# Transforms on 64 by 64 parts of TensorE's array, in one burst a group

## The chip, the cores and the metric

The kernel runs on one core of one Trainium2 chip. A core has a matrix engine (TensorE, PE in the profile, with its weight loads shown as PEld), a vector engine (VectorE, DVE), a scalar engine (ScalarE, ACT), a general engine (GpSimd, POOL) and SyncE (SP), which here only issues DMA transfers. The metric is the device time of one execution in microseconds. All data are 32-bit floats.

## What is computed

The reference filters a sequence in the frequency domain and feeds the result to a gated feed-forward block:

```python
X = np.fft.rfft(x, axis=1)              # x: 8 batches, 3008 tokens, 256 channels
Y = X * (filt_r + 1j * filt_i)[None]    # one complex factor for each of 1505 frequencies and channel
y = np.fft.irfft(Y, n=3008, axis=1)
t = y.reshape(8 * 3008, 256)
g = t @ w_gate                          # w_gate, w_val: 256 by 1536; w_out: 1536 by 256
out = (g / (1 + exp(-g)) * (t @ w_val)) @ w_out
```

The weights arrive as 64-bit floats, which the kernel rounds to 32 bits itself during the first batch.

## The kernel before

**Two streams of work.** The feed-forward part of batch b runs in 12 groups (four chunks of 752 tokens, three slices of the hidden units each, `NCHUNK` and `NG`). In the same groups the transform of batch b + 1 is made, so that it is ready when batch b ends. The last batch, having no follower, transforms nothing.

**The feed-forward part** multiplies with fewer products than the plain method takes. Sums of inputs (`y_t`) and sums of weights (`wt_t`) stand in for some of the products, and operations of VectorE, ScalarE and GpSimd put the results together. Its products are at L862 (PSUM tiles `wk`, `wa`, `we`: 188 columns) and, for the output projection, at L954 (`wA`, `wF`, `wG`: 376 columns). [...] Seven are one pool (`wps`, `bank`) that the feed-forward tiles use in turn, and one is apart (`fps`, `fbank`) and serves the transform.

**The transform** splits 3008 into 47 by 64. The first step makes a real 47-point transform for each of the 64 columns, 24 complex frequencies (48 numbers) each. The middle step takes, for each of the 24 frequencies, a 64-point transform with the twiddle factors in its matrix (128 by 128, for real and imaginary parts of 64 values), multiplies with the filter, and goes back with a second 128 by 128 matrix. The last step is 47 points back. Between the steps the data go through DRAM (`d1`, `d2`), which changes what lies on the 128 partitions.

From batch 2 on, the first step uses that the inputs of a real transform can be paired: `pair` (VectorE) makes sums and differences of rows n and 47 - n, and `stage1_paired` (L639, L641) takes five columns at once with a table of 120 rows and columns, 13 times. The middle step has 12 units (`stage2a`, `stage2b`), each for two frequencies: two matmuls of 128 by 128 by 256 columns at L698, three VectorE operations with the filter at L707, L711 and L714 (each reading PSUM), one addition on GpSimd (L716, shown at its helper's line, L256), two matmuls back at L731, one ScalarE copy (L739) and a transfer to `d2`. The filter is loaded for each unit from its inputs, in six transfers of 64 KB (L580). Batches 0 and 1 have transforms of their own: batch 0 before the groups begin, batch 1 (`stage1`, L658) during the groups of batch 0. The last step (`stage3`, L765) is made in groups 0, 1, 4, 7 and 11.

**The order is written out by hand.** The string `SCHEDULE` lists the operations of a group as tokens, and every instruction is put on its engine in that order (`pin`). [...] P, Q, A, B and E are products, W projections (those of the group before), f, c, x, s, y, e, m, l, g, u, h, v the operations between and after the products, S and D are GpSimd's, and o and z put projections into the output. A token `t2.1` is the place for piece 2, part 1 of the transform: a list `plan` says which units of the transform are the pieces of a group, and a unit is a Python generator whose parts run at successive tokens. A group thus has up to five pieces.

Of the kernel before, what the change touches and what calls it, by code (L numbers as in the profile page):

```python
# [41 lines left out]
FP32 = mybir.dt.float32  # L42
U32 = mybir.dt.uint32
# [15 lines left out]
NH = 4  # L59
# [13 lines left out]
NP = 5  # L73
NPAIR = N1 // 2
N_PAIRED = -(-N2 // NP)

# [12 lines left out]
Q0 o3' z1.o' t4.2' W2 f0 S00' S01' x0.o' t0.0 x1.o' Q1 t0.1 x2.o' P3 x3.o' f1 t4.3' W1 x4.o' S10' x03 S11'  # L89
s13 x5.o' P1 o1 t0.2 P0 o2 z0.o c1 D01 A13 g1 c0 S20' Q2 S21' g0 y01 m13 t1.0 h0 f2 s01 W6 t1.1 h1 x23  # L90
D02 P2 o6 D12 A01 c2 B13 g2 n3' m01 t0.3 S30' t1.2 x02 W7 S31' g13 y12 y02 B01 h13 o7 t1.3 t2.0 s02
s12 g01 h2 Q3 t2.1 h01 e12 A02 y23 W4 e02 y03 m02 g3 A12 o4 z2.o t2.2 E12 m12 B02 t2.3 l12 E02 u12 e13
g02 t3.0 h3 s23 l02 B12 v12 E13 t3.1 h02 u02 A23 n2 l13 g12 v02 W5 s03 e23 h12 e01 m23 A03 o5
# [8 lines left out]
""".split()  # L102
BLOCKS = (0, 1, 3, 2)
# [21 lines left out]
def dft_tables():  # L125
# [31 lines left out]
    paired = np.zeros((NP * (NPAIR + 1), 2, NP, NS))  # L157
    for j in range(NP):
        paired[NPAIR * j:NPAIR * (j + 1), :, j] = w[1:NPAIR + 1]
        paired[NP * NPAIR + j, 0, j] = 1.0  # L160
    paired = paired.reshape(NP * (NPAIR + 1), -1)


    pairs = np.arange(128).reshape(2, N2).T.ravel()
    later = np.stack([de[:, :, 0], de[:, :, 1][:, :, pairs]], 2)
    f32 = np.float32
    return (wf.reshape(NR, NK).astype(f32), wi.reshape(NK, NR).astype(f32),
            back.astype(f32), paired.astype(f32), np.ascontiguousarray(de).astype(f32),
# [4 lines left out]
def kernel(  # L173
# [11 lines left out]
    wf_host, wi_host, back_host, paired_host, de_host, later_host = dft_tables()  # L185
    wf_dram = nc.inline_tensor(wf_host, name="wf_tbl")
    wi_dram = nc.inline_tensor(wi_host, name="wi_tbl")
    paired_dram = nc.inline_tensor(paired_host, name="paired_tbl")
# [34 lines left out]

    def weights_of(b, k, g):
        return wt_1 if b == 0 and k < NT and g == 1 else wt_t
# [6 lines left out]
    w_dram = wdpool.tile([NG, 128, NPR, 2, 128], FP32, name="w_all")  # L232
    wo_t = cpool.tile([128, NJ, 7, 128], FP32)
# [19 lines left out]
    pin = tc.keep_in_program_order  # L253

# [3 lines left out]
    def sub(eng, dst, a, b):  # L258
        return eng.tensor_tensor(out=dst, in0=a, in1=b, op=ALU.subtract)  # L259
# [224 lines left out]
    back_t, paired_t, differences, third = [], [], [], []  # L484

    def load_back():

        for n in range(3):
            t = rpool.tile([128, 2, 128], U32, name=f"paired_{n}", tag="pw", bufs=3)
            t = t.bitcast(FP32).rearrange("p b f -> p (b f)")  # L490
            (differences if n else paired_t).append(t[0:NP * (NPAIR + (not n))])
        t = rpool.tile([128, 2, 128, 2], U32, name="x_third", tag="raw", bufs=2)
        t = t.bitcast(FP32).rearrange("p b f two -> p (b f two)")
        third.append(t[0:NP * (NPAIR + 1)].rearrange("p (i c) -> p i c", c=C))
        pin(nc.sync.dma_start(out=paired_t[0][:, 0:2 * NP * NS], in_=paired_dram.ap()))
        t = rpool.tile([128, 2, 128, 2], U32, name="back", tag="raw", bufs=2)
        t = t.bitcast(FP32).rearrange("p b f two -> p (b f two)")
        back_t.append(t[:, 0:10 * N1])
        pin(nc.sync.dma_start(out=back_t[0], in_=back_dram.ap()))
# [15 lines left out]
    class Spectral:  # L515
# [25 lines left out]
        def load_x(self, u):  # L541
            if self.b == 0:
                rows = x[0].rearrange("(r n) c -> r n c", n=32)
                for a, n in ((0, 4), (4, 4)):
                    for r in (slice(0, 80), slice(80, NR)):
                        self.load(out=x0[u][r, a:a + n, :],
                                  in_=rows[r, 8 * u + a:8 * u + a + n, :])
            elif self.b > 1:
                if u < N_PAIRED:
                    t = third[0]  # L550
                    if u % 3 < 2:
                        t = xpool.tile([NP * (NPAIR + 1), 2, C], FP32, name=f"x_{self.b}_{u}",
                                       tag="x")
                    n2, pairs = min(NP * u, N2 - NP), NP * NPAIR
                    rows = x[self.b].rearrange("(n1 n2) c -> n2 n1 c", n2=N2)
                    back = bass.AP(tensor=x.tensor,
                                   offset=x.offset + ((self.b * N1 + N1 - 1) * N2 + n2) * C,
                                   ap=[[C, NP], [-N2 * C, NPAIR], [1, C]])
                    self.load(out=t[0:pairs, 0], in_=rows[n2:n2 + NP, 1:NPAIR + 1])
                    self.load(out=t[0:pairs, 1], in_=back)  # L560
                    self.load(out=t[pairs:pairs + NP, 0], in_=rows[n2:n2 + NP, 0])
                    self.x[u] = t
            elif u < N_ONE:
                self.x[u] = xpool.tile([NR, NV, C], FP32, name=f"x_{self.b}_{u}", tag="x")
                rows = x[self.b].rearrange("(r n) c -> r n c", n=32)

                for r in (slice(0, 80), slice(80, NR)):
                    self.load(out=self.x[u][r], in_=rows[r, ts(u, NV), :])

        def load_two(self, u):  # L570
            if u < N_TWO:
# [10 lines left out]
                if self.b < 2:  # L582
                    self.load(out=self.t2[u], in_=self.twos(self.d1, u))
                    return
                rows = self.d1.rearrange("a n c -> (a n) c").rearrange(
                    "(n s p) c -> p n s c", n=N2, p=2)
                for i in range(2):
                    self.load(out=self.t2[u][N2 * i:N2 * (i + 1)], in_=rows[i, :, ts(u, NV)])
# [37 lines left out]
        def pair(self, u):  # L626

            if u < N_PAIRED:
                a, b = [self.x[u][0:NP * NPAIR, i] for i in range(2)]
                pin(sub(nc.vector, differences[u % 2], a, b))  # L630
                pin(add(nc.vector, a, a, b))

        def stage1_paired(self, u):

            t1 = t1pool.tile([NP * NS, 2, C], FP32, name=f"t1_{self.b}_{u}", tag="t1", bufs=2)
            ps = self.bank(f"pa_{self.b}_{u}")[0:NP * NS]
            table = paired_t[0]
            m = NP * NS
            pin(nc.tensor.matmul(out=ps[:, 0], lhsT=table[:, 0:m], rhs=self.x.pop(u)[:, 0],  # L639
                                 start=True, stop=True))  # L640
            pin(nc.tensor.matmul(out=ps[:, 1], lhsT=table[0:NP * NPAIR, m:2 * m],  # L641
                                 rhs=differences[u % 2], start=True, stop=True))
            self.load_x(u + 3)
            yield
            pin(nc.scalar.copy(out=t1, in_=ps))
            n2 = min(NP * u, N2 - NP)

            rows = self.d1.rearrange("a n c -> (a n) c").rearrange("(r p) c -> r (p c)", p=2)
            pin(nc.scalar.dma_start(out=rows[NS * n2:NS * (n2 + NP)],
                                    in_=t1.rearrange("p i c -> p (i c)")))  # L650
            yield
            self.pair(u + 2)
# [444 lines left out]
    older = before = None  # L1097
    pieces_before = []
# [52 lines left out]
    for b in range(B):  # L1151
# [8 lines left out]
        if b:  # L1160
            one = [nxt.stage1_paired(u) for u in range(N_PAIRED)] if nxt else []
        else:
            one = [nxt.stage1(u) for u in range(N_ONE)]
        two = []
        for u in range(N_TWO + 2) if nxt else ():
            two += [nxt.stage2b(u - 2)] if u > 1 else []
            two += [nxt.stage2a(u)] if u < N_TWO else []
        if nxt:
            plan[0] = one[0:2] + d[0][0:1] + one[2:3] + d[0][1:2]
            plan[1] = one[3:4] + d[0][2:3] + one[4:5] + d[0][3:4] + one[5:6]  # L1170
            plan[2], plan[3] = (one[6:10], one[10:13]) if b else (one[6:11], one[11:16])
            plan[4] = d[1] + two[0:1]

            plan[5], plan[6] = [iter(())] + two[1:5], two[5:10]
            plan[7] = two[10:11] + d[2]
            plan[8], plan[9] = two[11:16], two[16:21]
            plan[10], plan[11] = two[21:24], three(nxt, 0)
# [10 lines left out]
        for step in range(NCHUNK * NG + (b == B - 1)):  # L1188
# [16 lines left out]
            for place, token in enumerate(SCHEDULE):  # L1205
# [5 lines left out]
                if op[0] == "t":  # L1211
                    n = int(op[1])
                    ps = pieces_before if old else pieces
                    if n < len(ps):
                        next(ps[n], None)
                elif op[0] in "Wo" or op.endswith(".o"):
# [10 lines left out]
                if nxt and (step, op) == ((4, "P2") if b else (5, "A23")):  # L1227
                    nxt.load_two(0)
                if b + 2 < B and (step, op) in ((10, "Q2"), (10, "B01"), (11, "Q2")):

                    following.load_x(2 if step == 11 else int(op == "B01"))
                if b + 2 < B and step == 11 and op in ("A02", "B02"):
                    following.pair(int(op == "B02"))
# [43 lines left out]
```

## Time and profile before

The median of three runs is 2894.39 us (2893.86 to 2896.27). The profiled execution has a span of 2893.4 us, at a granted TensorE clock of 0.998 of full speed.

| what | value |
|---|---|
| chain of work that ended last | TensorE 89%, GpSimd 3%, VectorE 2% |
| DMA | mean 193 GB/s; 396368 packets, 201080 of them under 512 bytes |
| matmuls L639 and L641 (first step, batches 2 to 7) | 156 and 156 records, means of 379 and 378 ns |
| matmuls L698 and L731 (middle step, batches 1 to 7) | 336 and 336 records, means of 379 and 383 ns |
| copies L645 and L739 on ScalarE | 78 and 84, means of 586 and 585 ns |
| L707, L711, L714 on VectorE | 84 each, means of 691, 693 and 684 ns |
| additions of 128 by 512 on GpSimd (middle step) | 84, mean 1273 ns |
| pairs on VectorE, `x<-x`, `paired<-x`, `x_third<-x_third`, `paired<-x_third` | 54, 54, 24, 24; 36.6, 31.6, 27.9 and 16.7 us in all |

A row of the profile's groups names the line, the engine, the operation and the tiles (out<-in), then the shape and the number of records, the busy time in us, the mean of one in ns, and the idle time of the engine before them with what ended it. [...] the next one starts before it ends, so durations of matmuls do not add up to the time they take.

### The profile page before, as it was taken

Reading aid. Unit: us, or ns where it says so; the run is one execution under the profiler, and the core shown is the slowest. Engines: PE = TensorE matmul, PEld = TensorE weight load, DVE = VectorE, ACT = ScalarE, POOL = GpSimd, SP = SyncE. Lnnn points to the kernel's source line nnn. Section 1 sums busy time; section 2 is a strip of 40 time slices with the busy share of each in tenths; the row PEclk is TensorE's granted clock in tenths of the full one; section 3 lists DMA queues with packets and bytes.
Section 4 is the critical chain, followed back from the end, with each engine's and each line's share of the span. In section 5 each row is a group of like instructions: output and inputs, shape, how many; then the busy total and the mean of one; then the engine's idle time right before and its main releaser. Section 6 shows DMA issues by size and latency. Waiting matters only on the chain.

```text
span 2893.4 us, 47312 instructions
## 1 busy us (share of the span) xinstructions
PE 2843.6 (98%) x14784; PEld 2434.4 (84%) x14784; DVE 2073.4 (72%) x4664; ACT 1576.6 (54%) x4190; POOL 1532.2 (53%) x1669
## 2 busy tenths in 40 slices
PE   8999989999999999999999999999999999999998
PEld 6777778888888888888888888888888888888886
DVE  6888766776777767777767677677677767766666
ACT  6776445555555555555555554555555555555553
POOL 4886665454445554446453555444554544555443
PEclk9999999999999999999999999999999999999999
DMA  8687865666566665667656566566765666645443
GB/s 228 216 264 253 287 193 164 188 211 204 185 182 189 220 190 182 194 185 214 196 179 199 177 213 204 179 196 180 213 192 190 185 207 193 208 140 163 145 138 80
DMA packets 396368, 558.89 MB, mean 193 GB/s; under 512 B 201080, under 2 KB 296586, under 8 KB 396118
## 3 DMA queue, kind: packets, MB, share of 16 engines
q1 hardware_dynamic: 366533, 506.80, 57.7%
q10 hardware_dynamic: 27792, 45.72, 4.7%
q0 software_dynamic: 1792, 3.34, 0.4%
q8 instruction: 120, 1.97, 0.3%
q14 instruction: 131, 1.07, 0.1%
HBM read 460.38 MB, written 95.34 MB: 192 GB/s over the span
## 4 chain that ended last, share of the span: by engine, by line
PE 89%; POOL 3%; DVE 2%; issue 1%; ACT 0%; DMA 0%; POOLq 0%; DVEq 0%
PE wa L862 24%; PE wA L954 16%; PE wk L862 15%; PE we L862 12%; PE wG L954 8%; PE wF L954 4%; PE pd L765 3%; PE pc L731 3%; PE pb L698 2%; PE pa L639 1%; PE pa L641 1%; POOL out_dram L943 1%; POOL h L259 1%; POOL h L256 0%; DVE o L256 0%
## 5 line engine op out<-in xcount | busy, mean ns | idle before, releaser
L862 PE MATMUL wa<-y_t,wt_t 128*128 128x188 f32 x4464 | 879.0, 323 | 9.3 <-DVE wa L884 6.2
L862 PEld LDWEIGHTS wa<-y_t,wt_t 128*128 128x128 f32 x4464 | 748.7, 190 | 90.7 <-ACT wa L888 9.5
L256 POOL TENSOR_TENSOR h<-h 128x376 f32<-128x376 f32 x190 | 184.4, 992 | 778.1 <-DVE h L909 778.1
L862 PEld LDWEIGHTS wk<-y,wt_t 128*128 128x128 f32 x2976 | 501.0, 190 | 80.0 <-DVE y L256 0.5
L862 PE MATMUL wk<-y,wt_t 128*128 128x188 f32 x2976 | 565.0, 323 | 0.0
L259 POOL TENSOR_TENSOR h<-h 128x376 f32<-128x376 f32 x570 | 562.6, 1009 | 0.1
L954 PE MATMUL wA<-h,wo_t 128*128 128x376 f32 x1536 | 549.9, 480 | 9.0 <-POOL h L259 4.6
L862 PE MATMUL we<-y_t,wt_t 128*128 128x188 f32 x2232 | 431.6, 323 | 0.8 <-ACT we L893 0.7
L259 DVE TENSOR_TENSOR we<-we,m 128x376 f32<-128x376 f32 x576 | 316.5, 554 | 136.6 <-PE we L862 87.2
L954 PEld LDWEIGHTS wA<-h,wo_t 128*128 128x128 f32 x1536 | 279.3, 190 | 115.9 <-POOL h L259 8.6
L862 PEld LDWEIGHTS we<-y_t,wt_t 128*128 128x128 f32 x2232 | 369.4, 190 | 1.4 <-ACT we L893 1.0
L259 POOL TENSOR_TENSOR D<-f,f 128x376 f32<-128x376 f32 x288 | 280.9, 987 | 131.7 <-ACT f L877 123.2
L897 ACT COPY m<-wa 128x376 f32<-128x376 f32 x576 | 271.8, 472 | 86.7 <-PE wa L862 83.8
L263 DVE SCALAR_TENSOR_TENSOR y<-wk,c 128x376 f32<-128x376 f32 x480 | 243.7, 540 | 84.6 <-ACT we L893 56.0
L904 ACT ACTIVATE u<-we 128x188 f32<-128x188 f32 x576 | 188.7, 328 | 191.1 <-DVE we L259 171.2
L954 PE MATMUL wG<-h,wo_t 128*128 128x376 f32 x768 | 274.0, 479 | 1.2 <-DVE o L256 1.2
L904 ACT ACTIVATE g<-wa 128x188 f32<-128x188 f32 x576 | 187.3, 326 | 158.9 <-PE wa L862 143.2
L877 ACT ACTIVATE f<-wk 128x376 f32<-128x376 f32 x288 | 139.2, 483 | 223.7 <-PE wk L862 158.3
L881 ACT COPY c<-wk 128x376 f32<-128x376 f32 x288 | 136.0, 472 | 220.8 <-PE wk L862 220.8
L884 DVE SCALAR_TENSOR_TENSOR x<-wk,f 128x376 f32<-128x376 f32 x192 | 104.2, 543 | 201.7 <-PE wk L862 199.6
L893 ACT COPY we<-y 128x376 f32<-128x376 f32 x480 | 221.2, 479 | 39.6 <-DVE h L909 25.5
L909 DVE TENSOR_TENSOR h<-wa,g 128x188 f32<-128x188 f32 x576 | 196.4, 345 | 31.2 <-ACT g L904 30.3
(157 smaller groups left out, 3855.3 us busy)
## 6 DMA issues: line engine op xcount, KB each, us to landing
wt_t<-w_all SPq DMA_DIRECT2D x174, 896.0 KB
wt_t<-w_all SPq DMA_DIRECT2D x174, 768.0 KB
lent<-later_tbl SPq DMA_DIRECT2D x84, 256.0 KB
lent<-in_filt_r_dram SPq DMA_DIRECT2D x336, 64.0 KB
d<-lent ACTq DMA_DIRECT2D x84, 256.0 KB
d<-t ACTq DMA_DIRECT2D x78, 240.0 KB
lent<-d SPq DMA_DIRECT2D x144, 128.0 KB
t<-d SPq DMA_DIRECT2D x112, 128.0 KB
```

The source lines that it names most:

```text
L256: return eng.tensor_tensor(out=dst, in0=a, in1=b, op=ALU.add)
L259: return eng.tensor_tensor(out=dst, in0=a, in1=b, op=ALU.subtract)
L263: return nc.vector.scalar_tensor_tensor(out=dst, in0=a, scalar=-1.0, in1=b, op0=ALU.mult, op1=ALU.subtract)
L862: pin(nc.tensor.matmul(out=ps[:, z], lhsT=self.wt[:, SLOT[p], z], rhs=rhs, start=start and z == 0, stop=True, skip_group_check=True))
L877: pin(act.mul(self.small(f"f{i}", f"f{i}", 1), t[f"k{i}"], -1.0))
L881: pin(act.copy(out=self.small(f"c{i}", f"c{i}", 1), in_=t[f"k{i}"]))
L884: pin(v.scalar_tensor_tensor(out=dst, in0=t[f"k{j}"], scalar=-1.0, in1=t[f"f{i}" if j == 3 else f"D{at}"], op0=ALU.mult, op1=ALU.add))
L893: pin(act.copy(out=self.bank(f"e{at}"), in_=t[f"y{at}"]))
L897: pin(act.copy(out=self.small(f"m{at}", "m", 4), in_=t[f"a{at}"]))
L904: pin(act.activation(out=self.small(op, "g", 3, 1)[:, 0], in_=ps[:, 1], func=AF.Silu))
L909: pin(v.tensor_tensor(out=dst, in0=ps[:, 0], in1=g, op=ALU.mult))
L954: pin(nc.tensor.matmul(out=self.tiles[at], lhsT=wo_t[:, JB * q + i, WO[p], :], rhs=self.hs[i][:, HID[p]], start=start and i == 0, stop=Tru ...
```

## The change

The transforms of batches 2 to 7 are made in another way, and at other places of the order.

- **First step** (`quads`, groups 0 to 3). The 64 columns are taken as two halves, one on partitions 0 to 46, the other on 64 to 110. A tile of the array of 64 rows by 64 columns serves each half with its own 47 by 48 table (`quad`; that of the second half includes a turn). Two tiles of columns next to each other in the array take different columns of the input. The input comes in eight pieces of eight columns, two a group, which make eight matmuls of 512 columns each group, into four PSUM banks.
- **Middle step** (`fours`, groups 4 to 10). `halves` (VectorE) makes the sum and the difference of the two halves of 64 points; from these, the even and the odd of the 64 frequencies come with 64 by 64 matrices instead of one of 128 by 128. A unit has four of the 24 first-step frequencies: eight matmuls of 256 columns there into two banks and, one group later, eight home from two banks, joined by a subtraction and an addition on VectorE.
- **Filter product.** The results of the way there are copied to SBUF (ScalarE). Real and imaginary rows alternate there, and two DMA transfers exchange them into a second tile; VectorE multiplies both tiles with the filter's two parts (`tensor_tensor` and `scalar_tensor_tensor`), GpSimd adds.
- **Filter in DRAM.** `keep_filter` writes the filter once, early in batch 1, into a DRAM tile in the layout wanted (16 transfers). A unit then loads its part in one transfer of 1 MB.
- **Places.** Twelve tokens b0 to b11 in `SCHEDULE` run the parts of a group's burst: all its matmuls at b0, right behind W2 at the head of the group. The banks are of the shared pool of seven. The pieces t0 to t4 hold only the last step from batch 1 on.

The purpose is to let four 64 by 64 matmuls share the array, and to do the middle step with half the multiplications. The core of the diff:

```diff
-Q0 o3' z1.o' t4.2' W2 f0 S00' S01' x0.o' t0.0 x1.o' Q1 t0.1 x2.o' P3 x3.o' f1 t4.3' W1 x4.o' S10' x03 S11'
+Q0 o3' z1.o' t4.2' W2 b0 f0 S00' S01' b1 b2 x0.o' t0.0 x1.o' Q1 t0.1 x2.o' P3 x3.o' f1 t4.3' W1 x4.o' S10' x03 b3 S11'
...
+        def quads(self, g):
...
+                for cp in range(2):
+                    for h in range(2):
+                        r = slice(64 * h, 64 * h + N1)
+                        pin(nc.tensor.matmul(
+                            out=banks[u, h][64 * cp:64 * cp + 64], lhsT=quad_t[0][r, 0:64],
+                            rhs=xt[r, 2 * cp:2 * cp + 2].rearrange("p n c -> p (n c)"),
+                            start=True, stop=True))
...
+        def halves(self, e):
...
+            f = (add, sub)[e]
+            pin(f(nc.vector, self.sums[:, e], t[:, :, 0], t[:, :, 1]))
...
+        def fours(self, w):
...
+                for s in (0, 2, 1, 3):
+                    for e in range(2):
+                        r = slice(64 * e, 64 * e + 64)
+                        pin(nc.tensor.matmul(
+                            out=home[e][s // 2 * 64:s // 2 * 64 + 64, s % 2 * C:s % 2 * C + C],
+                            lhsT=tb[r, 1, 64 * s:64 * s + 64], rhs=y[r, s],
+                            start=s % 2 == 0, stop=True, skip_group_check=True))
...
+                for s in range(2):
+                    for e in range(2):
+                        for p in range(2):
+                            r = slice(64 * p, 64 * p + 64)
+                            a = 64 * (2 * s + e)
+                            pin(nc.tensor.matmul(
+                                out=there[p][64 * e:64 * e + 64, ts(s, C)],
+                                lhsT=tb[r, 0, a:a + 64], rhs=self.sums[r, e, s],
+                                start=s == 0, stop=True, skip_group_check=True))
+            yield
...
+                pin(nc.scalar.copy(out=z[:, 0], in_=home[0]))
+                pin(sub(nc.vector, z[:, 1], z[:, 0], home[1]))
...
+                pin(nc.scalar.copy(out=y[:, 0:2], in_=there[0].rearrange("p (s c) -> p s c", c=C)))
+            yield
...
+                pin(add(nc.vector, z[:, 0], z[:, 0], home[1]))
...
+                pin(nc.scalar.copy(out=y[:, 2:4], in_=there[1].rearrange("p (s c) -> p s c", c=C)))
...
+                for r in range(2):
+                    self.load(out=pairs[0][:, r], in_=pairs[1][:, 1 - r])
+                self.load_four(w + 1)
...
+                    pin(nc.vector.tensor_tensor(out=y[:, a], in0=y[:, a], in1=self.f[w][:, 0, a],
+                                                op=ALU.mult))
...
+                    pin(nc.vector.scalar_tensor_tensor(
+                        out=q[:, a], in0=q[:, a], scalar=quad_t[0][:, 64:65],
+                        in1=self.f[w][:, 1, a], op0=ALU.mult, op1=ALU.mult))
+                    pin(add(nc.gpsimd, y[:, a], y[:, a], q[:, a]))
...
+        if b and nxt:
+            for n in range(N_QUAD // 2):
+                bursts[n] = nxt.quads(n)
+            for n in range(N_FOUR + 1):
+                bursts[N_QUAD // 2 + n] = nxt.fours(n)
```

## The prediction

> **What bounds the kernel now.** I read the busy times first, then the same figures by stretch, then what TensorE waits for, then its pitch.
>
> ```profile
> PE 2843.6 (98%) x14784; PEld 2434.4 (84%) x14784; DVE 2073.4 (72%) x4664; ACT 1576.6 (54%) x4190; POOL 1532.2 (53%) x1669
> ```
>
> 98% busy alone says little, since ends of matmuls are modelled. Busy time by stretch, a middle batch and the last batch (which transforms no following batch):
>
> ```profile
> core 0: us, PE busy (x) PEld busy (x) DVE busy (x) ACT busy (x) POOL busy (x), PEclk, DMA share, GB/s
> 510.00:850.00 340.00, 339.71 (x1772) 293.46 (x1771) 243.75 (x547) 181.84 (x484) 177.84 (x184) 1.00 0.64 193
> 2590.00:2850.00 260.00, 260.00 (x1375) 225.24 (x1374) 172.60 (x414) 144.16 (x395) 127.89 (x138) 1.00 0.49 147
> ```
>
> TensorE is idle 0.29 us of 340 with the transforms and 0 of 260 without. The second row matters: the feed-forward part keeps TensorE full without transform matmuls between its products, so taking them away opens no holes by itself. The groups of TensorE work from 500 to 2850 us agree; the last figure is the idle time before them:
>
> ```profile
> L862 PE MATMUL wa<-y_t,wt_t 128*128 128x188 f32 x3924 | 771.6, 322 | 0.0
> L731 PE MATMUL pc<-lent 128*128 128x256 f32 x288 | 74.8, 382 | 1.8 <-DVE lent L714 1.0
> L698 PE MATMUL pb<-lent 128*128 128x256 f32 x288 | 73.9, 379 | 0.0
> ```
>
> The true price of a matmul is its pitch, start to start, in the timeline of TensorE:
>
> ```profile
> 1000.52 0.80 PE L862 MATMUL wa<-y_t,wt_t 128*128 128x188 f32 x4
> 1001.16 0.80 PE L862 MATMUL we<-y_t,wt_t 128*128 128x188 f32 x4
> 1001.79 1.03 PE L731 MATMUL pc<-lent 128*128 128x256 f32 x4
> 1002.66 0.80 PE L862 MATMUL wa<-y_t,wt_t 128*128 128x188 f32 x4
> 1004.57 1.43 PE L954 MATMUL wG<-h,wo_t 128*128 128x376 f32 x4
> 1005.83 0.80 PE L862 MATMUL wa<-y_t,wt_t 128*128 128x188 f32 x4
> ```
>
> Four records of 188 columns take 0.64 us (0.16 each), four of 256 take 0.87 (0.2175), four of 376 take 1.26 (0.315). By the slope from 256 to 376 (0.81 ns a column) one of 512 columns takes 0.2175 + 256 x 0.00081 = 0.425 us. Each fp32 matmul of the program stands as two records, one after the other (13 at L641 in each of 6 batches, but x156): two passes. From 500 us on, every microsecond of TensorE work added or removed is one of the run.
>
> [...] from the tile views (min/median/max ns):
>
> ```profile
> L256 DVE TENSOR_TENSOR x<-x x54: 424/426/1108, 441.0 to 2304.1; 115x256 f32<-115x256 f32 x54
> L256 DVE TENSOR_TENSOR x_third<-x_third x24: 426/1090/1494, 461.6 to 2293.4; 115x256 f32<-115x256 f32 x24
> ```
>
> The same addition takes 0.43 us alone and 1.09 beside GpSimd.
>
> **The change, part by part.** Only six transforms change, those of batches 2 to 7.
>
> TensorE, removed: L639 156 records, L641 156, and six sevenths of the 336 at L698 and of the 336 at L731 (288 each): 888 x 0.2175 = 193 us.
>
> TensorE, added: first step 32 matmuls a batch, 512 columns; middle step 48 there and 48 home, 256 columns. With two passes and six batches, 384 records of 0.425 and 1152 of 0.2175: 163 + 251 = 414 us if one runs at a time. All have 64x64 parts, neighbours in the order always on different parts, four in turn. The unknown is how many overlap:
> - all four: 414/4 = 103 us, net -90. [...]
> - in strict order: [...] only the second pass of one and the first of the next overlap: n matmuls take n + 1 passes. First step 24 bursts x 9 x 0.425 = 92; middle step (5 x 17 + 2 x 9) x 0.2175 x 6 = 134; 226 us, net +33.
> - none: 414, net +221.
>
> I take four: [...]
>
> Switching: 11 bursts a batch, 66, each with two changes of mode. The bounds: nothing, or a drain (a 376-column matmul's 0.480 less its pitch 0.315: 0.165) plus a weight load not hidden (1001.64 to 1001.79 in the timeline: 0.15), so 132 x 0.315 = 42 us. I take half, 21.
>
> VectorE, for each batch. Removed: three operations of 0.69 us in 12 units at L707 to L714 (24.8) and the pairs, 112.8/6 = 18.8 by the four rows of `x`, `x_third` and `paired`; 43.6 together. Added: 8 evacuations of 512 columns (0.69, like L707), 12 more reading the home banks, and 36 with two SBUF inputs: 0.69 alone, about 1.35 beside GpSimd (0.66 longer, as above). GpSimd is busy half the time: 1.02. Sum 20 x 0.69 + 36 x 1.02 = 50.5: little more in sum, but 6 x 1.02 + 2 x 0.69 = 7.5 us fall in each of six groups, and they run up to 9.5. Two groups without transform, from the last batch:
>
> ```profile
> 2614.00:2640.00 26.00, 26.00 (x137) 22.30 (x136) 17.56 (x42) 13.91 (x39) 17.85 (x19) 1.00 0.54 167
> 2640.00:2665.00 25.00, 25.00 (x133) 21.60 (x132) 18.67 (x44) 13.26 (x38) 11.91 (x14) 1.00 0.41 135
> ```
>
> 18.7 + 7.5 = 26.2 of about 27.2 us (25 + burst of 1.74 + switching): 96%; 17.6 + 7.5 of 28.2: 89%. What that costs is seen in the first batch:
>
> ```profile
> 170.00:200.00 30.00, 28.78 (x138) 22.36 (x137) 26.33 (x60) 24.09 (x67) 20.69 (x31) 1.00 0.92 309
> 200.00:230.00 30.00, 30.00 (x145) 23.78 (x144) 24.82 (x58) 21.52 (x58) 18.26 (x27) 1.00 0.84 281
> 230.00:260.00 30.00, 28.71 (x139) 22.55 (x138) 27.37 (x57) 18.59 (x52) 23.65 (x29) 1.00 0.68 221
> ```
>
> VectorE at 83% costs TensorE nothing, at 88% and 91% 1.2 to 1.3 us. 36 groups, some half of them in that state: 18 x 1.25 = 22 us; bounds 0 and 36 x 1.25 = 45.
>
> ScalarE loses 25 copies of 512 columns a batch and gets 26: nothing. GpSimd keeps 12 additions of 512. Filter: 36 loads of 1 MB in place of 432 of 64 KB (six sevenths of 504); the 16 transfers that write the copy run in the first two groups of batch 1, where the DMA engines are busy 0.64 of the time, and nothing reads it before the fourth. I cost both at nothing.
>
> New waits. The burst takes four of the seven shared PSUM banks. It stands behind W3, Q0 and W2 (4 x 0.315 + 4 x 0.16 + 4 x 0.315 = 3.2 us), in which g03, h03, u03, v03 (0.33 to 0.35 each) empty the last banks; behind it, P3 waits for the first copy (0.59) of a bank filled half a burst (0.87) earlier, with Q1 (0.64) between, and W1 for two VectorE operations more, with P3 (0.64) between: about even, nothing to 0.3 us. The exchange of real and imaginary rows by DMA is issued at b4 and read at b7, 39 of the order's 166 places or some 6 us later; if late, VectorE stops and m, l, v and h behind it. I count both as nothing; the upper ends lie in the range.
>
> Sum: -90 + 21 + 22 = -47, 2894 to **2847 us**.
>
> **Rivals.**
> - Strict order: +33 + 21 = +54, 2948. For it: [...] two passes per matmul on one part. [...] Slower.
> - Four parts overlap, but VectorE is the bound: at 9.5 us a group, 18.7 + 9.5 = 28.2 against 27.2, and later waits; with 2 us lost in each of 36 groups, -90 + 21 + 72 = +3, 2897. For it: 1090 ns above. Against: GpSimd is busy only half the time.
> - No overlap: +221 + 21, 3136.
> - Switching and waits free: -90, 2804.
>
> **How the numbers follow.** Four overlap with the middle costs, 0.56 together with the free end: 2804 to 2885. VectorE the bound 0.10, half of it within 0.2%. Strict order 0.29, 2930 to 2975. None 0.05. Range 2812 to 2955: nearly all of the first, all of the second, over half of the third. Faster 0.56, same 0.05, slower 0.05 + 0.29 + 0.05 = 0.39.
>
> **What would show it.** In the trace after, a middle-step burst of 16 matmuls should last 1.7 to 2.4 us from its first start to the next feed-forward matmul (strict order: 3.7; none: 7). Gaps of up to 0.3 us at both edges would be the switching. TensorE's waits should name VectorE in the six groups of the middle step. Wrong would be: bursts of 3.7 us, or bursts of 1.7 us and more than 2 us idle in each of those groups.

## The result and the profile after

The changed kernel takes **2944.95 us** (median; 2943.18 to 2946.97), the kernel before 2895.33 on the same chip: a ratio of **1.0172 [1.0154, 1.019]**, some 50 us slower. Forecast was a gain of 47. The first line of the profile after, busy times of the engines:

```profile
PE 2822.3 (96%) x15432; PEld 2324.9 (79%) x15432; DVE 2080.4 (71%) x4628; ACT 1567.0 (53%) x4196; POOL 1551.0 (53%) x1669
```

There are 648 more matmul records (1536 added, 888 removed) and less busy time, 2822.3 for 2843.6 us; the share falls from 98% to 96%. So TensorE does get less work; it now waits. The stretch that holds the six changed transforms shows the same, first before, then after (columns: busy time of each engine, with the number of records; then granted clock, DMA share, GB/s):

```profile
440.00:2520.00 2080.00, 2076.27 (x10834) 1794.69 (x10833) 1490.41 (x3360) 1118.52 (x2971) 1063.89 (x1105) 1.00 0.64 194
```

```profile
440.00:2560.00 2120.00, 2046.98 (x11443) 1678.51 (x11442) 1496.81 (x3314) 1101.73 (x2961) 1077.96 (x1101) 0.99 0.65 202
```

TensorE is idle 3.7 us before and 73.0 after. VectorE's sum hardly moves (1490 to 1497): what changes is when it can work. The last batch, without transforms, is idle for nothing, as before:

```profile
2650.00:2900.00 250.00, 250.00 (x1318) 216.25 (x1317) 166.67 (x399) 137.58 (x378) 122.34 (x132) 1.00 0.49 148
```

**Where in a batch.** The same view for four groups of one batch: of the first step; with the middle step there and home (two of these); and one near the end, past the exchanges:

```profile
1239.00:1267.00 28.00, 28.00 (x153) 22.78 (x152) 19.11 (x44) 14.95 (x40) 17.81 (x18) 1.00 0.68 209
1355.00:1385.00 30.00, 28.28 (x164) 22.44 (x163) 24.86 (x52) 15.05 (x41) 15.91 (x17) 1.00 0.63 208
1385.00:1420.00 35.00, 32.15 (x188) 27.12 (x187) 22.74 (x49) 17.67 (x46) 13.27 (x15) 0.95 0.68 202
1481.00:1507.00 26.00, 26.00 (x146) 21.69 (x145) 16.50 (x39) 15.24 (x41) 9.94 (x12) 1.00 0.76 209
```

The first and the last lose nothing though the first has a full burst. The loss is in the groups that have the exchange and the filter product. The third row is not the one with the fullest VectorE (22.74 of 35 us, 65%), yet it has the most idle time, and its clock falls to 0.95.

**What TensorE waits for** from 440 to 2560 us (us in all, times, longest):

```profile
PE wa L1027 <- DVE wa L1049: 49.9, 33, 4.3
PE wA L1119 <- DVE o L309: 14.3, 23, 0.6
PE pd L930 <- DMA t<-d: 4.0, 1, 4.0
```

The same wait before the change, from 440 to 2520 us:

```profile
PE wa L862 <- DVE wa L884: 1.4, 1, 1.4
```

The first line after the change names VectorE 33 times; the stretch has 36 groups with the exchange and the filter product. But VectorE at L1049 is only the messenger. What VectorE itself waits for, from 580 to 2560 us:

```profile
DVE lent L312 <- ACT lent L769: 95.6, 34, 3.0
DVE x L1049 <- PE wk L1027: 66.0, 61, 4.1
DVE lent L797 <- DMA lent<-lent: 62.8, 34, 5.7
```

The first two rows are ordinary waits for data: both stay (96.3 and 72.6 us) in the first experiment below, where the loss is gone. The third is new: the first multiplication with the filter (L797) waits for the exchange of real and imaginary rows. One group in order of time shows the whole chain (start us, duration us; the engine with q is a DMA queue; brackets give idle time and what ended it):

```profile
1354.75 1.43 PE L1119 MATMUL wF<-h,wo_t 128*128 128x376 f32 x4
1356.11 1.09 PE L748 MATMUL wqc<-lent 64*64 64x256 f32 x16
1357.02 1.04 PE L759 MATMUL wqb<-lent 64*64 64x256 f32 x16
1358.00 1.54 PE L1027 MATMUL wk<-y,wt_t 128*128 128x188 f32 x8
...
1358.64 0.59 ACT L777 COPY lent<-wqb 128x512 f32<-128x512 f32 x1
...
1359.26 1.13 SPq L579 DMA_DIRECT2D lent<-lent  x2
...
1364.29 1.34 DVE L797 TENSOR_TENSOR lent<-lent 128x512 f32<-128x512 f32 x1 [0.97 <-DMA lent<-lent]
1365.55 0.34 DVE L1074 TENSOR_TENSOR h<-wk,g 128x188 f32<-128x188 f32 x1
1365.82 0.54 DVE L1049 SCALAR_TENSOR_TENSOR wa<-wk,D 128x376 f32<-128x376 f32 x1
1366.41 1.54 PE L1027 MATMUL wa<-y_t,wt_t 128*128 128x188 f32 x8 [1.01 <-DVE wa L1049]
```

The burst of 16 matmuls (32 records) lasts from 1356.11 to 1358.00, 1.89 us. The copy that completes `y` ends at 1359.23 and the exchange is issued. VectorE has other work until 1363.32; then it comes to token b5 and, taking its operations in the written order, stands for 0.97 us until the exchange has landed, at 1364.29. The operation there lasts 1.34 us, L1049 (token s01) comes behind it, and TensorE's `wa` product waits 1.01 us for that.

It is worse where output leaves, in two groups of a batch. The queue of SyncE and its effect, 30 us later:

```profile
1385.85 8.97 SPq L1108 DMA_DIRECT2D out_dram<-o  x12
1394.91 1.16 SPq L579 DMA_DIRECT2D lent<-lent  x2
...
1397.92 0.69 DVE L797 TENSOR_TENSOR lent<-lent 128x512 f32<-128x512 f32 x1 [4.26 <-DMA lent<-lent]
1399.39 2.87 PE L1027 MATMUL wa<-y_t,wt_t 128*128 128x188 f32 x8 [2.85 <-DVE wa L1049]
```

Twelve output transfers take 9 us to issue, the exchange stands behind them in the same queue, and TensorE loses 2.85 us in one wait. The `wa` line is 2.87 us long for eight records that take 1.54 in the group above: from 1399 to 1402 us the granted clock is 0.50. Not every pause has this beside it: after one of 3.05 us, which ends at 1045.11, the clock stays at 1.00 and the eight records take 1.54. Over the whole run the granted clock is 0.991 (before 0.998).

Why does the wait fall on the *first* multiplication, which doesn't use the exchanged tile? It writes its product into `y`, in place, and the exchange is still reading `y`: in the run where it writes another tile (below), the 62.8 us of this wait are gone from its line. The prediction looked for the reader of the exchanged tile (L803, at b7); the wait comes from the writer of the tile that the exchange reads.

### The profile page after: what moved, and what is told of

Same layout as the page of the kernel before. It is cut to its first block, busy times and chain, and to the rows that moved or that the text cites. A ratio compares the mean times of both kernels' runs of the same rounds, so it can differ in the third digit from the quotient of the medians.

```text
span 2943.1 us, 48249 instructions
## 1 busy us (share of the span) xinstructions
PE 2822.3 (96%) x15432; PEld 2324.9 (79%) x15432; DVE 2080.4 (71%) x4628; ACT 1567.0 (53%) x4196; POOL 1551.0 (53%) x1669
## 5 line engine op out<-in xcount | busy, mean ns | idle before, releaser
L1027 PE MATMUL wa<-y_t,wt_t 128*128 128x188 f32 x4464 | 894.9, 327 | 60.6 <-DVE wa L1049 54.5
L1119 PE MATMUL wA<-h,wo_t 128*128 128x376 f32 x1536 | 562.4, 489 | 22.7 <-DVE o L309 17.3
L1027 PEld LDWEIGHTS wk<-y,wt_t 128*128 128x128 f32 x2976 | 495.1, 190 | 108.0 <-DVE lent L682 19.5
L1027 PE MATMUL wk<-y,wt_t 128*128 128x188 f32 x2976 | 572.1, 325 | 1.1 <-DMA wt_t<-w_all 1.1
L309 POOL TENSOR_TENSOR h<-h 128x376 f32<-128x376 f32 x190 | 183.1, 985 | 739.6 <-DVE h L1074 739.6
L312 POOL TENSOR_TENSOR h<-h 128x376 f32<-128x376 f32 x570 | 572.3, 1023 | 0.1
L1074 DVE TENSOR_TENSOR h<-we,u 128x188 f32<-128x188 f32 x576 | 198.3, 345 | 32.1 <-ACT u L1069 21.4
L1074 DVE TENSOR_TENSOR h<-wa,g 128x188 f32<-128x188 f32 x576 | 198.4, 345 | 29.8 <-ACT g L1069 29.2
```

The costliest lines, as they stand in the source:

```text
L309: return eng.tensor_tensor(out=dst, in0=a, in1=b, op=ALU.add)
L1027: pin(nc.tensor.matmul(out=ps[:, z], lhsT=self.wt[:, SLOT[p], z], rhs=rhs, start=start and z == 0, stop=True, skip_group_check=True))
L1074: pin(v.tensor_tensor(out=dst, in0=ps[:, 0], in1=g, op=ALU.mult))
L1119: pin(nc.tensor.matmul(out=self.tiles[at], lhsT=wo_t[:, JB * q + i, WO[p], :], rhs=self.hs[i][:, HID[p]], start=start and i == 0, stop=Tru ...
```

## The experiments

Theory A: the exchange must land by b5 and comes too late. Theory B: the second multiplication and the addition beside it, VectorE's added work, are too much. The experiments ran on three chips; the kernel before took 2897.47 us beside the first four, 2895.38 beside the next four and 2895.75 beside the last two. Ratios are to the kernel before on the same chip.

### The filter product later in the group

The tokens after b4 move back: b5 to the old place of b7, b6 to that of b8, b8 to that of b9; b7 and b9 to places further on. Work is the same.

```diff
-s13 x5.o' P1 o1 b4 t0.2 P0 o2 z0.o c1 D01 A13 g1 c0 S20' Q2 S21' g0 y01 m13 t1.0 b5 h0 f2 s01 W6 t1.1 h1 x23
-D02 P2 b6 o6 D12 A01 c2 B13 g2 n3' m01 t0.3 S30' t1.2 b7 x02 W7 S31' g13 y12 y02 B01 h13 o7 t1.3 t2.0 b8 s02
-s12 g01 h2 Q3 t2.1 h01 e12 A02 y23 W4 e02 y03 m02 g3 A12 o4 z2.o t2.2 b9 E12 m12 B02 t2.3 l12 E02 u12 e13
+s13 x5.o' P1 o1 b4 t0.2 P0 o2 z0.o c1 D01 A13 g1 c0 S20' Q2 S21' g0 y01 m13 t1.0 h0 f2 s01 W6 t1.1 h1 x23
+D02 P2 o6 D12 A01 c2 B13 g2 n3' m01 t0.3 S30' t1.2 b5 x02 W7 S31' g13 y12 y02 B01 h13 o7 t1.3 t2.0 b6 s02
+s12 g01 h2 Q3 t2.1 h01 e12 A02 y23 W4 b7 e02 y03 m02 g3 A12 o4 z2.o t2.2 b8 E12 m12 B02 t2.3 l12 b9 E02 u12 e13
```

> The filter multiplications (b5 to b8) and the loads behind them (b9) stand some 20 places later in the order; nothing else is changed. Theory A, VectorE stands at b5 because the in-place multiplication must wait until the exchange by DMA has read its tile: the waits of TensorE for VectorE at L1049 (54.5 us) and L309 (17.3 us) go, 2840 to 2870 us. Theory B, VectorE is too full in these six groups (operations slowed beside GpSimd): the same operations, so 2935 to 2950.

2872.94 us, ratio **0.9916 [0.9901, 0.993]**: from slower than before to faster. TensorE's waits from 440 to 2600 us:

```profile
PE wa L1027 <- ACT wa L1053: 9.0, 12, 0.8
PE we L1027 <- DVE we L316: 8.8, 13, 1.0
PE pd L930 <- DMA t<-d: 4.7, 1, 4.7
```

The 49.9 us for L1049 are gone. By place alone, 0.0256 of 2895 us comes back, 74 us. VectorE still waits for the exchange at L797 (21.1 us in ten waits, 62.8 us in the changed kernel), but TensorE no longer waits for what stands behind. Theory A missed its 2840 to 2870 by 3 us; theory B's 2935 to 2950 is far off.

### Without the exchange

The two transfers are left out (the second tile keeps old contents); every multiplication and every place stays.

```diff
                 pairs = [t.rearrange("(q r) s c -> q r s c", r=2) for t in (q, y)]
-                for r in range(2):
-                    self.load(out=pairs[0][:, r], in_=pairs[1][:, 1 - r])
                 self.load_four(w + 1)
```

> The two transfers that exchange real and imaginary rows are left out (the second multiplication then reads old data); everything else stands where it was. Theory A: nothing to wait for at b5, 2840 to 2870 us. Theory B: 2935 to 2950.

2868.66 us, ratio **0.9899 [0.9883, 0.9916]**, 79 us less than the changed kernel. TensorE's largest waits:

```profile
PE wA L1117 <- DVE o L309: 12.0, 24, 0.5
PE pd L928 <- DMA t<-d: 4.2, 1, 4.2
```

Keeping the transfers and moving the multiplications, and leaving the transfers out, bring the same within 6 us. So the price of the exchange is its place, not its traffic.

### Without the second multiplication

L803 and the GpSimd addition that follows it are left out; exchange and places stay.

```diff
                 if there:
-                    pin(nc.vector.scalar_tensor_tensor(
-                        out=q[:, a], in0=q[:, a], scalar=quad_t[0][:, 64:65],
-                        in1=self.f[w][:, 1, a], op0=ALU.mult, op1=ALU.mult))
-                    pin(add(nc.gpsimd, y[:, a], y[:, a], q[:, a]))
+                    pass
```

> The second multiplication (L803, 72 operations of 1193 ns, 86 us of VectorE) and the addition on GpSimd that follows it are left out; the exchange and the first multiplication stay. Theory A: the wait at b5 stays, and only part of the later waits goes: 2905 to 2940 us. Theory B: VectorE has 2.4 us less in each of the groups, and GpSimd no longer slows the rest: 2840 to 2880.

2924.07 us, ratio 1.0091 [1.0076, 1.0106]: still slower than before. First TensorE's wait, then VectorE's:

```profile
PE wa L1024 <- DVE wa L1046: 45.9, 33, 3.0
```

```profile
DVE lent L797 <- DMA lent<-lent: 63.0, 36, 4.4
```

Both waits stand nearly as they were (49.9 and 62.8 us in the changed kernel), although nothing reads the exchanged tile any more. So it is not its reader that waits; the first multiplication, which is left with its write into `y`, does. Theory B is refuted as the main cause. The 21 us below the changed kernel are what the two operations cost with the wait still in place; they don't measure how full VectorE is.

### The exchange from ScalarE's queue

```diff
-                    self.load(out=pairs[0][:, r], in_=pairs[1][:, 1 - r])
+                    pin(nc.scalar.dma_start(out=pairs[0][:, r], in_=pairs[1][:, 1 - r]))
```

> The exchange is issued from ScalarE's queue and not from SyncE's, where 4 to 12 output transfers stand ahead of it in two of the six groups. Theory C, the lateness is the place in the queue: nearly all stalls go, 2845 to 2880 us. Theory A with the transfer's own 3 to 4 us as the cause: only what the two groups lose above the others goes (about 1 us in the group at step 4, 1.5 in that at step 7, six times each): 2925 to 2940.

2960.87 us, ratio 1.0216 [1.0199, 1.0233]: slower than either theory said, and slower than the changed kernel. VectorE's waits, then ScalarE in order of time:

```profile
DVE y L316 <- ACT c L1046: 70.5, 58, 2.7
DVE lent L797 <- DMA lent<-lent: 51.5, 34, 3.0
```

```profile
1368.95 1.32 ACTq L783 DMA_DIRECT2D d<-lent  x2
1370.37 1.96 ACTq L791 DMA_DIRECT2D lent<-lent  x2
1372.37 0.47 ACT L1046 COPY c<-wk 128x376 f32<-128x376 f32 x1 [3.13 <-DVE o L1095]
```

The queue's effect is as meant: the longest wait at L797 falls from 5.7 to 3.0 us. But four issues hold ScalarE 3.3 us, the copy of `c` behind them is late, and VectorE's wait for it grows from 31.8 us in the changed kernel to 70.5. (The bracket names another releaser for ScalarE; the issues that fill its time are the lines above.) A wait was shortened on one engine and a longer one made on another.

### The filter written a batch earlier

```diff
-                if b == 1 and step < 2 and op in FILTER_AT:
-                    keep_filter(8 * step + FILTER_AT.index(op))
+                if b == 0 and step > 9 and op in FILTER_AT:
+                    keep_filter(8 * (step - 10) + FILTER_AT.index(op))
```

> The changed kernel with one edit: the 16 transfers that write the filter to DRAM run in the last two groups of batch 0 and not in the first two of batch 1. If they were what made TensorE wait 5.1 us for two other transfers in the first group of batch 1 (and 3.5 us in shorter gaps there): 2934 to 2941 us against 2945. If that wait has another cause, or the transfers do the same harm in batch 0: 2943 to 2950.

2933.94 us, ratio 1.0136 [1.0117, 1.0155], some 10 us less than the changed kernel (0.0036 of 2895). In the stretch from 440 to 580 us the wait for `t<-d`, 4.0 us in the changed kernel, is

```profile
PE pd L930 <- DMA t<-d: 1.3, 1, 1.3
```

The prediction counted the writing at nothing. Some 2.7 us of the gain is this wait. The clock has a part too: from 486 to 526 us the granted clock is 0.87 in the changed kernel (0.50 from 498 to 508) and 1.00 here. Groups 0 and 1 of batch 1, in which the writing stood, take 67.4 us together in the changed kernel and 61.3 here, 6 us less. The other 4 us weren't traced; the four times of this kernel lie 14 us apart, and its trace is of the longest.

### Both: product later, filter earlier

> The filter multiplications later in the order (as in e1_later, 2873 us) and the filter written early: both edits are apart, so the sum, 2862 to 2868 us; 2873 if the writing costs nothing.

2862.73 us, ratio 0.9889 [0.9874, 0.9904], 8 us below the first experiment by the ratios, as the sum of the two asks. The next kernel is the first experiment's with another order inside the bursts; it ran on the same chip as this one and is only 3 us slower, so the early filter is worth 3 to 10 us by whole times.

### One part of the array after the other

In the first experiment's kernel, the order of the matmuls inside a burst: all of one 64 by 64 part, then the next part.

```diff
-                for s in (0, 2, 1, 3):
-                    for e in range(2):
+                for e in range(2):
+                    for s in range(4):
...
-                for s in range(2):
-                    for e in range(2):
-                        for p in range(2):
+                for p in range(2):
+                    for e in range(2):
+                        for s in range(2):
```

> e1_later (2873 us) with another order inside the bursts of the middle step: the matmuls of one 64 by 64 part stand together, four passes in a row on each part, and not one matmul on each part in turn. If passes wait at their own part without holding back those behind them: 2870 to 2880. If only one pass can be parked at a part, [...] of the 16 passes of eight matmuls some 12 to 13 lie one after the other: 2.7 us and not 0.9 for each eight, 12 times in each of six batches: 2980 to 3010.

2865.85 us, ratio 0.9898 [0.9882, 0.9915]: 4 us under the first range, the same as the first experiment's within the intervals, and far from the second range. A burst of it:

```profile
1325.72 1.43 PE L1119 MATMUL wF<-h,wo_t 128*128 128x376 f32 x4
1327.08 1.11 PE L748 MATMUL wqc<-lent 64*64 64x256 f32 x16
1327.99 1.11 PE L759 MATMUL wqb<-lent 64*64 64x256 f32 x16
1329.03 1.54 PE L1027 MATMUL wk<-y,wt_t 128*128 128x188 f32 x8
```

1.95 us, against 1.89. Strict order, as the prediction counts it, would let only the last pass of one part and the first of the next overlap: 8 runs of four passes, 8 x 3 + 1 = 25 passes of 0.2175 (the pitch before the change), 5.4 us, an estimate. So in these bursts the overlap does not need neighbours on different parts. Taken one by one in the trace, the 16 records at L748 begin in sets of four, some 0.22 us from set to set, in this kernel as in the changed one (13 ns apart within a set here, 7 there), although the first four passes as written are all on one part. The records don't name their part; that TensorE took later parts ahead is inferred from this, not seen.

### Sums and differences on GpSimd

The both-edits kernel, with `halves` moved from VectorE to GpSimd.

```diff
-            pin(f(nc.vector, self.sums[:, e], t[:, :, 0], t[:, :, 1]))
+            pin(f(nc.gpsimd, self.sums[:, e], t[:, :, 0], t[:, :, 1]))
```

> e6_later_early with the sums and differences of halves (72 operations of 0.69 us) on GpSimd and not on VectorE. Theory A' : what is left of the loss in the six groups (about 1.6 us in each of four of them) is VectorE being full in the second half of a group: 2840 to 2855 us. Rival: GpSimd takes 1.27 us for each [...], so the sums of h that wait behind them on GpSimd and the other operations of VectorE are late: 2862 to 2890.

2847.72 us, ratio 0.9838 [0.9823, 0.9852], 15 us less. With the exchange out of the way, VectorE's fullness is at least 15 us of what remains; TensorE's waits for `wa` (10.3 us in the kernel it starts from) are down to 1.3, and its largest are

```profile
PE we L1027 <- DVE we L316: 8.6, 14, 0.7
PE pd L930 <- DMA t<-d: 1.4, 1, 1.4
```

### The first product out of place

The changed kernel, with the first multiplication writing another tile; all places stay.

```diff
-                    pin(nc.vector.tensor_tensor(out=y[:, a], in0=y[:, a], in1=self.f[w][:, 0, a],
+                    pin(nc.vector.tensor_tensor(out=v[:, a], in0=y[:, a], in1=self.f[w][:, 0, a],
...
-                    pin(add(nc.gpsimd, y[:, a], y[:, a], q[:, a]))
+                    pin(add(nc.gpsimd, y[:, a], v[:, a], q[:, a]))
```

> The changed kernel with one edit: the first multiplication writes another tile (the room of the results home) and not the tile that the exchange is reading; GpSimd's addition reads it there. Order, exchange and number of operations are as in the changed kernel (2945 us). If VectorE stands at b5 only because the in-place write must wait for the exchange's read: the wait for the exchange moves to b7, where it has mostly landed, but the room written is itself read by the transfer to d2, issued at about the same time as the exchange and landing in 3.9 us and not 2.7, so some of the wait may stay under another name: 2880 to 2915 us. If the wait is not that of the write, 2940 to 2950.

2914.08 us, ratio 1.006 [1.0045, 1.0075]. VectorE's wait at the first multiplication, then TensorE's wait (one line was added, so L797 is now L798):

```profile
DVE lent L798 <- DMA d<-lent: 38.2, 28, 3.0
```

```profile
PE wa L1028 <- DVE wa L1050: 27.6, 26, 2.4
```

The wait for the exchange is gone at this line (at the second multiplication 5.1 us of it are left), as it should be if writing `y` was the cause. A shorter one stands in its place, since the tile taken is read by the transfer to `d2` of the same burst. TensorE's 49.9 us fall to 27.6. By groups, the gain lies in the two that have output ahead in SyncE's queue: group 4 takes 29.8 to 30.1 us in place of 30.5 to 33.7, group 7 takes 31 to 32 in place of 34 to 38. Groups 5, 6, 8 and 9 gain nothing: 30.2 us and more, mostly 30.2 to 30.4 in both kernels. A dependence on a transfer's *source* is again the limit.

### The parts spread further

The kernel with `halves` on GpSimd, and the last parts of the product spread wider: b7 to the old place of b9, b8, b9 and b10 into the line after.

```diff
-s12 g01 h2 Q3 t2.1 h01 e12 A02 y23 W4 b7 e02 y03 m02 g3 A12 o4 z2.o t2.2 b8 E12 m12 B02 t2.3 l12 b9 E02 u12 e13
-g02 t3.0 b10 h3 s23 l02 B12 v12 E13 t3.1 h02 u02 A23 n2 b11 l13 g12 v02 W5 s03 e23 h12 e01 m23 A03 o5
+s12 g01 h2 Q3 t2.1 h01 e12 A02 y23 W4 e02 y03 m02 g3 A12 o4 z2.o t2.2 b7 E12 m12 B02 t2.3 l12 E02 u12 e13
+b8 g02 t3.0 b9 h3 s23 b10 l02 B12 v12 E13 t3.1 h02 u02 A23 n2 b11 l13 g12 v02 W5 s03 e23 h12 e01 m23 A03 o5
```

> e8_halves_pool (2848 us) with the second multiplications (b7, b8) and the steps behind them some ten places later, so that VectorE's operation for e13 (L316), for which TensorE waits 8.6 us, stands ahead of the second of them. If that wait goes and no other takes its place: 2836 to 2842 us. If VectorE is only crowded elsewhere: 2846 to 2860.

**2842.07 us** (2840.16 to 2843.22), ratio **0.9813 [0.9797, 0.983]**: it beats both kernels. The stretch corresponding to the two above:

```profile
440.00:2460.00 2020.00, 2015.96 (x11447) 1666.93 (x11446) 1432.79 (x3239) 1099.65 (x2965) 1156.48 (x1173) 1.00 0.69 210
```

TensorE is idle 4.0 us, about as before the change (3.7); the granted clock is 0.998 over the run.

## Why the prediction was wrong

**Four parts overlap: right.** The prediction took 1.7 to 2.4 us for a middle-step burst, and 3.7 in strict order. That four overlap was the author's estimate: the kernel before has no matmul on 64 by 64 parts. Measured: 1.89, where 32 records of 0.2175 us one at a time would make 7.0. First-step bursts, 16 records of 512 columns (1.70 at the best), agree:

```profile
524.71 1.43 PE L1119 MATMUL wF<-h,wo_t 128*128 128x376 f32 x4
526.07 1.95 PE L673 MATMUL wqa<-lent,quad 47*64 47x512 f32 x16
...
527.95 1.22 PE L1027 MATMUL wk<-y,wt_t 128*128 128x188 f32 x6
```

527.95 less 526.07 is 1.88 us, where 16 records of 0.425 one at a time would make 6.8. The strict-order rival (2948 us) came within 3 us of the measured time by a mechanism that neither the burst nor the reordered one shows: a matching sum is no evidence for its terms.

**Switching at 21 us: about right.** It was an estimate. The bursts exceed the pure stream (1.74 and 1.70 us, by the pitches before the change) by 0.15 and 0.18. A whole group shows more. From one `wF` product to the next, a group of the first step without products of the last step takes 27.47 us (from 1239.35), and a group of the last batch, without transforms, 25.40 (from 2609.92). So a full burst costs 2.07 us, some 0.35 beyond its stream; 66 times 0.35 is 23 us.

**VectorE's fullness at 22 us: too small, if anything.** The same count gives what groups 4 to 9 of the six batches, 36 groups, lose: their time, less 25.40 us, less 2.07 for a full burst (1.22 for a half one, as in group 10), less 0.80 for each six records of the last step (in the last batch a group with 24 of them takes 28.60). This is an estimate from these traces:

| kernel | lost in the 36 groups, us |
|---|---|
| changed | 111 |
| product later | 40 |
| without the exchange | 35 |
| both edits | 39 |
| and `halves` on GpSimd | 22 |
| and parts spread | 17 |

So 35 to 40 us are left when the exchange is out of the way, where the prediction had 22. Moving `halves` brought 15 us by whole times and spreading the parts 7 (0.0025 of 2895): these 22 are VectorE's load and order. The prediction's 1.25 us for a crowded group came from two stretches of the first batch, in which VectorE is named for only 1.4 of the 2.5 us that TensorE waits. The price of the second multiplication was taken as 1.02 us; from 580 to 2560 us the groups show 1.19 for it and 0.99 for the first (columns: busy us and mean ns; idle us and what ended it):

```profile
L803 DVE SCALAR_TENSOR_TENSOR lent<-lent,quad 128x512 f32<-128x512 f32 x72 | 85.9, 1193 | 0.0
L797 DVE TENSOR_TENSOR lent<-lent 128x512 f32<-128x512 f32 x72 | 71.4, 991 | 69.1 <-DMA lent<-lent 62.8 <-DMA lent<-d 6.4
```

Beside GpSimd such operations are slower: of the 54 additions `x<-x` before the change, the 30 with GpSimd idle take 0.42 to 0.43 us, the 24 others 0.69 to 1.11.

**The step that failed: "The exchange ... is issued at b4 and read at b7 ... I count both as nothing".** It named the right sequel ("VectorE stops and m, l, v and h behind it") but the wrong place and so the wrong time. The exchange has to be done at b5, since L797 overwrites its source. b5 stands 17 places behind b4, not 39: under 3 us by the step's own rate. From `y` complete (1359.23) to VectorE's start (1364.29) it takes 5 us, of which 1.13 is issue. In two groups of each batch the issue also stands behind output in SyncE's queue, which the step did not ask. Worth: 74 us by moving the product, 79 by leaving the exchange out (71 and 76 by the table).

**Filter writing at nothing: mis-sized.** By whole times 3 to 10 us; in groups 0 and 1 of batch 1, 6.

The sum: -90 + 23 for switching + 111 in the 36 groups (71 to 76 of it the exchange) + 9 in group 1 of batch 1 (38.3 us in place of 29.1; 6 of it the filter) makes +53; measured +50. Of the 120 us lost, 69 show as new idle time of TensorE, and 0.007 of clock in 2943 us is about 21 us more. Some 30 us show as neither; ends of matmuls are modelled, so short waits can hide behind them. The best kernel also loses some 17 us in the 36 groups and shows only 4.0 us idle.

**The test for wrong that the prediction set** was not met to the letter. The bursts last 1.9 us, below its 2.4, but "more than 2 us idle in each of those groups" holds in 9 of the 36; the mean is 1.9. TensorE's waits name VectorE, as it said, which by itself would have pointed to its rival "VectorE is the bound". That rival has the engine right and most of the reason wrong: in the worst group VectorE was busy for 22.74 us of 35 and waited for the exchange.

What stays open: what the last 17 us in the 36 groups wait for, and why whole times give the early filter anything from 3 to 10 us.

## What to carry to other kernels

In these runs a transfer within SBUF held up the next write of its source (62.8 us in 34 waits of the changed kernel), not only the readers of its target: count the time to the next *write of the source*, not only to the first read of the result, and ask what stands ahead of it in its queue. When a trace names an engine as the one waited for, look at that engine's own waits before calling it full: here its operations stood behind one that waited for a DMA, and moving the waiting multiplications some 20 places later, with the same work, turned 1.0172 into 0.9916. Moving an issue to another queue was not free here: four issues held ScalarE 3.3 us. And a low sum of idle time is no proof that nothing is lost; the time of like groups, with and without the change, showed more.

## What was not expected of the hardware

- Order within a burst made next to no difference to the overlap of 64 by 64 parts: 1.95 us with four passes of one part together, 1.89 with parts in turn. A strict order would have taken 5.4 us by the estimate above, and these two runs show no such cost.
- Some pauses have a lower clock beside them. In the group with the 2.85 us wait the granted clock is 0.95, and eight records of 188 columns last 2.87 us instead of 1.54; after a pause of 3.05 us in an earlier batch they last 1.54. What decides between the two is not shown.
- Two exchange transfers and two to `d2`, issued from ScalarE's queue, held that engine from 1368.95 to 1372.33, about 0.8 us each; SyncE issued its two in 1.13 us.
